# Splitting expert weights in a fused attention and MLP kernel: 24-bit words, rounded by ScalarE, low part by subtraction

## The chip, the cores and the metric

The kernel runs on one core of one Trainium2 chip. The metric is the device time of one launch in microseconds. A core has five engines with a queue each: TensorE (PE, matmuls; its weight loads are listed apart as PEld), VectorE (DVE), ScalarE (ACT), GpSimd (POOL) and SyncE (SP, which here only starts DMAs). Each engine works through its own instructions in order, and engines wait for each other on semaphores.

## The reference

Sink-window attention feeds a two-layer MLP with a squared ReLU.

```python
scores = (1.0 / np.sqrt(D)) * np.matmul(q, k.transpose(0, 1, 3, 2))   # q, k, v: (4, 8, 768, 64)
keep = is_sink | in_window                        # 4 sink keys, a causal window of 128
scores = np.where(keep, scores, -1000000000.0)
scores = scores - np.max(scores, axis=-1, keepdims=True)
a = np.exp(scores)
a = a / (np.sum(a, axis=-1, keepdims=True) + 1e-09)
x = np.matmul(a, v)                               # laid out as (3072, 512)
h = np.maximum(x @ w_in, 0.0)                     # w_in (512, 2048)
out = (h * h @ w_out).astype(np.float32)          # w_out (2048, 512), result (3072, 512)
```

The weights `w_in` and `w_out` arrive as float64 and are read by the kernel as pairs of 32-bit words: `low` (word 0) and `top` (word 1, with sign, exponent and the upper mantissa). 1e-9 is `EPS` in the kernel.

## The kernel before, in words

The 3072 tokens are eight chunks of 384; a chunk has four pairs of heads. For each pair, `score` (L233) makes scores on PE, takes the masked row maximum on DVE (the custom operation of L261, called the reduction here) and the exponential with its row sum on ACT (L264). `normalise` (L268) adds `EPS` to the sums, takes the reciprocal on DVE (L278) and lets POOL scale the probabilities (L289) and copy the sink columns (L302, L303). A tail then transposes the probabilities on PE (L358), copies them out of PSUM on ACT (L365) or DVE (L363), and does the same for the sink keys (`sink_keys`, L313, L314). `values` (L391) multiplies by v (L406, L409) and splits the result into a high part (ACT, L417) and a low part (DVE, L418).

`moe` (L453) yields the MLP in quanta, four to a block of 128 hidden columns: twelve matmuls of the first layer (L465), ReLU and squares on ACT (L476, L479, L481), a low part of the squares on DVE (L488), nine matmuls of the second layer (L503). Each weight is used as a high and a low part, both of the type fp32r, so a weight must be split before its first use.

`split_steps` (L564) splits one row, 128 partitions by 512 weights; there are 32 rows, 16 of each matrix, in the list `order`. A row is loaded by `load_row` (L558) into one of four buffers, two rows ahead. Before the change the row takes five passes on DVE and two on ACT:

- L573 and L575 (DVE): the top word is shifted and its sign and exponent bits are put back, which gives a float32 with 11 mantissa bits, `t1`;
- L577 (ACT) and L578 (DVE): the remaining bits are gathered as two 16-bit halves into an integer `m`;
- L580 (DVE): the exponent of `t1` alone, `eb`;
- L586 (ACT): `t1` is copied as the high part; L587 (DVE): the low part is `m * 2^-36 * eb`.

The order of the work is set in three ways. Up to the end of the first MLP leg (chunk 0, blocks 0 to 7) PE, DVE, ACT, POOL and SP follow the program's own order (`manual_schedule`). First come the pairs of chunk 0, `s` = 0 to 3, and a first pair of chunk 1, `s` = 4; between their parts `fill(1)` runs one step of the splitting, a step ending at each `yield`: fifteen such steps, five to a row before the change. To keep PE occupied there, `busy` (L638) issues matmuls on a zero tile. Then follows the loop of 32 quanta (`QUANTA`), called the loop here: each takes one quantum of the MLP, one item of the attention of chunk 1 (`todo`), and `fill(3)` or `fill(2)` steps of splitting. By its end 17 rows (`EARLY`) are split. After that, the other 15 rows (`split_row`, L590), the rest of the MLP and the attention of chunks 2 to 7 are ordered by the tile framework's planner by priorities.

Of the kernel before, what the change touches and what calls it, by code (L numbers as in the profile page):

```python
# [8 lines left out]
F32 = mybir.dt.float32  # L9
F32R = mybir.dt.float32r  # L10
I32 = mybir.dt.int32
U16 = mybir.dt.uint16
U32 = mybir.dt.uint32
BF16 = mybir.dt.bfloat16
AF = mybir.ActivationFunctionType
ALU = mybir.AluOpType
# [3 lines left out]
P = 128  # L20
# [6 lines left out]
WR = 512  # L27
# [7 lines left out]
EPS = 1.0e-9  # L35


def f32(ap):
    return ap.bitcast(F32)
# [3 lines left out]
def sink_window_attention_moe(  # L43
# [11 lines left out]
    nc = tc.nc  # L55
    B, NPAIR, _, S = q.shape
# [12 lines left out]
    with ExitStack() as fast:  # L69
        wp = fast.enter_context(tc.tile_pool(name="wp", bufs=1))  # L70
        ap1 = fast.enter_context(tc.tile_pool(name="ap1", bufs=1))
# [3 lines left out]
        op = fast.enter_context(tc.tile_pool(name="op", bufs=3))  # L75
# [23 lines left out]
        nc.gpsimd.iota(coli, pattern=[[1, P]], base=0, channel_multiplier=0)  # L99
        rel = op.tile([P, 2 * P], F32, tag="ob", name="rel")  # L100
        nc.vector.tensor_copy(rel, reli)
        far = ap1.tile([P, 2 * P], F32, tag="m", name="far")
        nc.vector.tensor_scalar(far, rel, 0.0, BIG, op0=ALU.is_lt, op1=ALU.mult)
        nc.vector.tensor_tensor(rel, rel, far, op=ALU.max)
        col = mp.tile([P, P], F32, tag="gl", name="col")
# [162 lines left out]
        def normalise(c, p, heads):  # L268
            st = state[c, p]
            half = c % NHALF  # L270
            i0 = 1 if half == 0 else 0
            hs = slice(heads[0], heads[-1] + 1)
            rs = ap2.tile([P, 2, NQ], F32, tag="rs", name=f"rs_{c}_{p}_{heads[0]}")
            if c > 1:
                nc.scalar.activation(rs[:, hs], st["sm"][:, hs], AF.Copy, bias=EPS)
            else:
                nc.vector.tensor_scalar(rs[:, hs], st["sm"][:, hs], EPS, None, op0=ALU.add)
            nc.vector.reciprocal(rs[:, hs], rs[:, hs])  # L278
            for hh in heads:
                Pt = st["P"][hh]  # L280
                j0 = 1 if half == 0 else 0
                if c > 1:

                    nc.gpsimd.tensor_tensor(  # L284
                        Pt[:, j0:NQ, 0:P], Pt[:, j0:NQ, 0:P], Pt[:, j0:NQ, BS:BAND], op=ALU.add
                    )
                for j in range(NQ):
                    n = P if j < j0 else (BS if c > 1 else BAND)
                    nc.gpsimd.tensor_scalar(  # L289
                        Pt[:, j, 0:n], Pt[:, j, 0:n], rs[:, hh, j : j + 1], 1.0, op0=ALU.mult, op1=ALU.mult  # L290
                    )
                own = slice(hh * NS, hh * NS + NS)
                src = Pt[:, i0:NQ, P:BS]
                if c > 1 and half == 1:

                    to = PSK[0].rearrange("p q c -> p (q c)")[:, 0 : NQ * 4 * NS]
                    to = to.rearrange("p (q t c) -> p q t c", t=2, c=2 * NS)
                    nc.gpsimd.tensor_copy(to[:, :, 0, own], src)
                    nc.gpsimd.tensor_tensor(to[:, :, 1, own], src, f32(to[:, :, 0, own]), op=ALU.subtract)
                    continue  # L300
                to = PSK[p % 2 if c < 2 else 0].rearrange("p q (t c) -> p q t c", c=2 * NS)[:, 0 : NQ - i0]
                nc.gpsimd.tensor_copy(to[:, :, 0:3:2, own], src.unsqueeze(2).broadcast_to([P, NQ - i0, 2, NS]))  # L302
                nc.gpsimd.tensor_tensor(to[:, :, 1, own], src, f32(to[:, :, 0, own]), op=ALU.subtract)  # L303
# [245 lines left out]
        NROW = len(order)  # L549
        HALF = NROW // 2  # L550
        AHEAD = 2
        raws = {}
# [5 lines left out]
        def load_row(n):  # L558
            if n in raws or n >= NROW:
                return  # L560
            raws[n] = wp.tile([P, WR, 2], I32, tag=f"wo{NFC - 4 + n % 4}", name=f"raw_{n}")
            nc.sync.dma_start(out=raws[n].rearrange("p (a w) t -> p a (w t)", a=NCC), in_=row_of(n))

        def split_steps(n):  # L564
            kind, j = order[n]
            load_row(n)
            top = raws[n][:, :, 1]
            words = raws[n].rearrange("p w t -> p (w t)").bitcast(U16).rearrange("p (w t) -> p w t", t=4)
            t1 = ap2.tile([P, WR], I32, tag="t1", name=f"t1_{n}")
            m = ap1.tile([P, WR], I32, tag="m", name=f"m_{n}")  # L570
            eb = ap1.tile([P, WR], I32, tag="eb", name=f"eb_{n}")
            m16 = m.bitcast(U16).rearrange("p (w t) -> p w t", t=2)
            nc.vector.tensor_scalar(t1, top, 3, 0x3FFFF000, op0=ALU.logical_shift_left, op1=ALU.bitwise_and)  # L573
            yield
            nc.vector.scalar_tensor_tensor(t1, top, -0x40000000, t1, op0=ALU.bitwise_and, op1=ALU.bitwise_or)  # L575
            yield
            nc.scalar.copy(m16[:, :, 0], words[:, :, 1])  # L577
            nc.vector.tensor_scalar(m16[:, :, 1], words[:, :, 2], 0x1FF, None, op0=ALU.bitwise_and)  # L578
            yield
            nc.vector.tensor_scalar(eb, t1, -0x800000, None, op0=ALU.bitwise_and)  # L580
            yield
            if kind == "i":
                row = wi[:, j]
            else:
                row = wo[j] = wp.tile([P, 2, DM], F32R, tag=f"wo{j}", name=f"wo_{j}")
            nc.scalar.copy(row[:, 0, :], f32(t1))  # L586
            nc.vector.scalar_tensor_tensor(row[:, 1, :], m, 2.0**-36, f32(eb), op0=ALU.mult, op1=ALU.mult)  # L587
            load_row(n + AHEAD)

        def split_row(n):  # L590
            keep = tc.cur_priority
# [5 lines left out]
        def check_row(n):  # L597

            keep = tc.cur_priority
            half = ap2.tile([P, WR // 2, 2], I32, tag="t1", name=f"half_{n}")  # L600
            sq = ap1.tile([P, WR // 2], BF16, tag="m", name=f"sq_{n}")
            src = row_of(n // 2)[:, n % 2 * 2 : n % 2 * 2 + 2]
            nc.sync.dma_start(out=half.rearrange("p (a w) t -> p a (w t)", a=2), in_=src)
            tc.cur_priority = keep + 12
            first = nc.scalar.activation(sq, f32(half[:, :, 1]), AF.Square, accum_out=wchk[:, 0, n : n + 1])
            tc.keep_in_program_order(first)
            nc.scalar.activation(sq, sq, AF.Relu, bias=theta, scale=-1.0, accum_out=wchk[:, 1, n : n + 1])
            tc.cur_priority = keep
# [4 lines left out]
        split = []  # L613

        def row_steps():
            for n in range(NROW):
                yield from split_steps(n)
                split.append(n)
                yield

        FH = NFC // 2
        legs = [(0, 0, FH), (1, 0, FH), (0, FH, NFC), (1, FH, NFC)] + [(c, 0, NFC) for c in range(2, NCHUNK)]
# [2 lines left out]
        EARLY = HALF + 1  # L625
        with tc.manual_schedule(engines={E.PE, E.DVE, E.Activation, E.Pool, E.SP}):
            steps = row_steps()

            def fill(n):
                for _ in range(n):  # L630
                    if len(split) < EARLY:
                        next(steps)
# [103 lines left out]
            for n in range(QUANTA):  # L736
                next(products)

                if todo:
                    todo.pop(0)()  # L740
                fill(3 if n % 4 == 0 else 2)
            while len(split) < EARLY:
                next(steps)
            for f in todo:
# [273 lines left out]
```

## Time and profile before

| | before |
|---|---|
| device time, median of 3 runs | 701.94 us (700.20 to 702.62) |
| device time of the profiled execution | 702.43 us |
| its span, first to last instruction | 700.7 us |
| PE busy / DVE busy / ACT busy / POOL busy | 686.8 / 430.5 / 439.3 / 228.1 us |
| granted TensorE clock, mean | 0.997 of full speed |

The profile lists for each engine its instructions with start, duration and, in square brackets, the idle time before it and what ended that. Durations of neighbours on one engine overlap a little at their ends, so the distance of two starts is what an instruction costs its queue. PE counts as busy also while a matmul waits inside its pipeline, so PE's share of busy time does not show by itself that it is at its limit.

### The profile page before, as it was taken

The numbers are of one execution on the slowest core, as the hardware profiler recorded it, in microseconds if no ns is written. First come the engines' busy times: TensorE is split into PE (matmuls) and PEld (weight loads), VectorE is DVE, ScalarE is ACT, GpSimd is POOL, SyncE is SP. The second block draws the span as 40 slices with busy tenths as digits, with TensorE's granted clock in tenths as the row PEclk, the third lists the DMA queues.
The fourth block names the chain that finished last, engine by engine and source line by source line (L and its number), as shares of the span: only waits on it lengthen the run. The fifth ranks groups of instructions, "written<-read, shape, count | busy, mean of one in ns | idle before, by whom it ended". The sixth has DMA issues, their size and how long they took to land.

```text
span 700.7 us, 11725 instructions
## 1 busy us (share of the span) xinstructions
PE 686.8 (98%) x3862; PEld 594.1 (85%) x3862; DVE 430.5 (61%) x1181; ACT 439.3 (63%) x1240; POOL 228.1 (33%) x433
## 2 busy tenths in 40 slices
PE   9899999999999999999999999999999999999995
PEld 4667789998888888888889888888988889889994
DVE  7789889946667666565566665666556665542221
ACT  6788877845666766676667777667676544422221
POOL 5664400034564432342343443233244242200000
PEclk9999999999999999999999999999999999999998
DMA  7476656511424423332435432243443210010001
GB/s 211 134 239 188 183 191 208 171 50 61 131 74 141 103 82 106 108 111 83 118 91 148 125 90 85 85 139 95 114 100 79 75 44 15 1 37 10 1 0 51
DMA packets 47268, 71.51 MB, mean 102 GB/s; under 512 B 4384, under 2 KB 30752, under 8 KB 47200
## 3 DMA queue, kind: packets, MB, share of 16 engines
q1 hardware_dynamic: 47056, 70.55, 34.8%
q8 instruction: 33, 0.54, 0.3%
q14 instruction: 35, 0.29, 0.1%
q10 hardware_dynamic: 144, 0.13, 0.1%
HBM read 62.80 MB, written 7.86 MB: 101 GB/s over the span
## 4 chain that ended last, share of the span: by engine, by line
PE 86%; ACT 2%; DVE 0%; issue 0%
PE po L503 36%; PE ph L465 36%; PE xo L406 5%; PE s L257 5%; PE pt L376 2%; PE xo L409 1%; ACT PTF L365 0%; ACT m L577 0%; ACT P L264 0%; PE pt L358 0%; PE pss L317 0%; PE pss L323 0%; ACT ph L481 0%; ACT ph L476 0%; ACT wi L586 0%
## 5 line engine op out<-in xcount | busy, mean ns | idle before, releaser
L465 PE MATMUL ph<-x,wi 128*128 128x384 f32 x1536 | 305.8, 340 | 0.0
L465 PEld LDWEIGHTS ph<-x,wi 128*128 128x128 f32 x1536 | 265.1, 188 | 9.1 <-issue 1.0
L503 PE MATMUL po<-wo,gh 128*128 128x512 f32 (+1 forms) x770 | 244.2, 398 | 0.0
L225 POOL TENSOR_TENSOR KS<-kn,KS 128x408 fp32r<-128x408 f32 (+1 forms) x48 | 58.8, 1226 | 317.8 <-ACT KS L224 317.8
L503 PEld LDWEIGHTS po<-wo,gh 128*128 128x128 f32 x770 | 136.0, 188 | 19.1 <-issue 1.6
L503 PE MATMUL po<-wo,gl 128*128 128x512 f32 x385 | 151.6, 394 | 0.0
L264 ACT ACTIVATE P<-P,nbs 128x264 f32<-128x264 f32 (+1 forms) x192 | 94.3, 491 | 74.3 <-DVE nbs L261 73.8
L484 DVE TENSOR_TENSOR ph<-ph,r 128x384 f32<-128x384 f32 x96 | 54.0, 563 | 76.7 <-ACT r L476 76.6
L261 DVE CUSTOM_DVE_ANT_0 P<-s,masks 128x264 f32<-128x264 f32 x160 | 67.1, 430 | 52.3 <-PE s L257 49.5
L289 POOL TENSOR_SCALAR P<-P,rs 128x136 f32<-128x136 f32 (+2 forms) x192 | 88.2, 475 | 31.6 <-DVE rs L278 23.4
L476 ACT ACTIVATE r<-ph 128x384 f32<-128x384 f32 x96 | 46.8, 487 | 77.6 <-PE ph L465 74.9
L503 PEld LDWEIGHTS po<-wo,gl 128*128 128x128 f32 x385 | 72.2, 188 | 16.1 <-DVE gl L488 0.2
L488 DVE TENSOR_TENSOR gl<-ph,gh 128x384 fp32r<-128x384 f32 x128 | 71.1, 555 | 23.5 <-ACT ph L481 12.0
L227 DVE TENSOR_TENSOR QS<-qn,QS 64x384 fp32r<-64x384 f32 x48 | 44.3, 922 | 24.4 <-ACT QS L226 24.0
L257 PE MATMUL s<-KS,QS 128*128 128x264 f32 (+1 forms) x288 | 56.9, 280 | 0.0
L284 POOL TENSOR_TENSOR P<-P 128x256 f32<-128x256 f32 (+1 forms) x48 | 48.4, 1009 | 24.9 <-ACT P L264 24.4
L257 PEld LDWEIGHTS s<-KS,QS 128*128 128x128 f32 x288 | 51.9, 188 | 5.0 <-DVE nbs L261 0.5
L479 ACT ACTIVATE gh<-r 128x384 fp32r<-128x384 f32 x96 | 50.3, 524 | 2.1
L382 DVE TENSOR_TENSOR PTF<-pt,halves 128x256 f32<-128x256 f32 x96 | 36.3, 419 | 22.1 <-PE pt L376 21.5
L406 PE MATMUL xo<-PTF,vn 128*64 128x256 f32 x448 | 45.9, 342 | 0.5 <-ACT PTF L365 0.5
L406 PEld LDWEIGHTS xo<-PTF,vn 128*64 128x64 f32 x448 | 31.2, 136 | 17.2 <-issue 9.3
L224 ACT CAST KS<-kn 128x408 fp32r<-128x408 f32 (+1 forms) x48 | 28.2, 589 | 24.5 <-issue 12.2
(108 smaller groups left out, 674.5 us busy)
## 6 DMA issues: line engine op xcount, KB each, us to landing
raw<-in_moe_w_in_dram SPq DMA_DIRECT2D x16, 512.0 KB, 3.9
raw<-in_moe_w_out_dram SPq DMA_DIRECT2D x16, 512.0 KB, 3.8
half<-in_moe_w_in_dram SPq DMA_DIRECT2D x32, 256.0 KB, 2.8
half<-in_moe_w_out_dram SPq DMA_DIRECT2D x32, 256.0 KB, 3.7
kn<-in_k_dram SPq DMA_DIRECT2D x24, 272.0 KB, 4.2
qn<-in_q_dram SPq DMA_DIRECT2D x32, 192.0 KB, 3.7
out_dram<-ob SPq DMA_DIRECT2D x23, 256.0 KB, 2.5
kn<-in_k_dram SPq DMA_DIRECT2D x24, 204.0 KB, 3.6
```

Source lines behind the costliest of these rows:

```text
L225: nc.gpsimd.tensor_tensor(KS[:, 1, 0:nk], st["kn"][:, hh, 0:nk], f32(KS[:, 0, 0:nk]), op=ALU.subtract)
L257: nc.tensor.matmul(ps[:, 0:n], st["QS", hh][:, qcols], flat[:, a, c0 : c0 + n], start=(a == 0), stop=(a == 1))
L261: nc.vector.tensor_tensor_reduce(Pt[:, i, 0:n], ps[:, 0:n], mask[:, 0:n], -SCALE, BIG, ALU.add, ALU.min, nb)
L264: nc.scalar.activation(Pt[:, i, 0:n], Pt[:, i, 0:n], AF.Exp, bias=nb, scale=-1.0, accum_out=sm[:, i : i + 1])
L284: nc.gpsimd.tensor_tensor(Pt[:, j0:NQ, 0:P], Pt[:, j0:NQ, 0:P], Pt[:, j0:NQ, BS:BAND], op=ALU.add)
L289: nc.gpsimd.tensor_scalar(Pt[:, j, 0:n], Pt[:, j, 0:n], rs[:, hh, j : j + 1], 1.0, op0=ALU.mult, op1=ALU.mult)
L406: nc.tensor.matmul(xo[h * D : h * D + D, cols], lhsT, rhs, start=(n == 0), stop=False, skip_group_check=True)
L465: nc.tensor.matmul(ph[:, 0:TOK], wi_at(i, cc, fc), xt[:, cc, :], start=(m == 0), stop=(m == 3 * NCC - 1),)
L479: nc.scalar.activation(gh, r, AF.Square)
L484: nc.vector.tensor_tensor(ph[:, 0:TOK], ph[:, 0:TOK], r, op=ALU.mult)
L488: late = lambda: nc.vector.tensor_tensor(gl, ph[:, 0:TOK], f32(gh), op=ALU.subtract)
L503: nc.tensor.matmul(po[t][:, e], gt[:, ts_], wo[f][:, i, e], start=(f == f0 and j == 0), stop=(f == f1 - 1 and j == 2), skip_group_check=True,)
```

## The change

The row is split in another way. The top word is shifted and masked with three more bits kept (L573's successor), the sign and exponent are put back as before, and a third pass joins the upper three bits of the low word, shifted right by 29: `t1` is now a float32 word with all 24 bits. ACT's copy of `t1` to fp32r rounds it, and the low part is the difference of the word and its rounded high part, a subtraction on DVE. So a row takes four passes on DVE and one on ACT; the tiles `m` and `eb` of the splitting are gone, and the two small users of the buffer tag `m` get a tag of their own (`far`).

A row now has four steps. `row_steps` is written anew: the first step of a row comes before the last step (the subtraction) of the row ahead of it. The load of the row two ahead is issued in the third step. The number of steps for each quantum goes from three in the first of four and two in the others (nine in four) to one in the last of four and two in the others (seven in four). In `normalise`, `EPS` is added by ACT for all chunks; before, DVE did it for chunks 0 and 1.

```diff
-            if c > 1:
-                nc.scalar.activation(rs[:, hs], st["sm"][:, hs], AF.Copy, bias=EPS)
-            else:
-                nc.vector.tensor_scalar(rs[:, hs], st["sm"][:, hs], EPS, None, op0=ALU.add)
+            nc.scalar.activation(rs[:, hs], st["sm"][:, hs], AF.Copy, bias=EPS)
             nc.vector.reciprocal(rs[:, hs], rs[:, hs])
...
-            nc.vector.tensor_scalar(t1, top, 3, 0x3FFFF000, op0=ALU.logical_shift_left, op1=ALU.bitwise_and)
+            nc.vector.tensor_scalar(t1, top, 3, 0x3FFFFFF8, op0=ALU.logical_shift_left, op1=ALU.bitwise_and)
             yield
             nc.vector.scalar_tensor_tensor(t1, top, -0x40000000, t1, op0=ALU.bitwise_and, op1=ALU.bitwise_or)
             yield
-            nc.scalar.copy(m16[:, :, 0], words[:, :, 1])
-            nc.vector.tensor_scalar(m16[:, :, 1], words[:, :, 2], 0x1FF, None, op0=ALU.bitwise_and)
-            yield
-            nc.vector.tensor_scalar(eb, t1, -0x800000, None, op0=ALU.bitwise_and)
-            yield
+            nc.vector.scalar_tensor_tensor(t1, low, 29, t1, op0=ALU.logical_shift_right, op1=ALU.bitwise_or)
...
             nc.scalar.copy(row[:, 0, :], f32(t1))
-            nc.vector.scalar_tensor_tensor(row[:, 1, :], m, 2.0**-36, f32(eb), op0=ALU.mult, op1=ALU.mult)
             load_row(n + AHEAD)
+            yield
+            nc.vector.tensor_tensor(row[:, 1, :], f32(t1), f32(row[:, 0, :]), op=ALU.subtract)
...
         def row_steps():
-            for n in range(NROW):
-                yield from split_steps(n)
-                split.append(n)
+            last = iter(())
+            for n in range(EARLY):
+                row = split_steps(n)
+                next(row)
                 yield
+                for _ in last:
+                    pass
+                if n > 0:
+                    split.append(n - 1)
+                    yield
+                next(row)
+                yield
+                next(row)
+                yield
+                last = row
+            for _ in last:
+                pass
+            split.append(EARLY - 1)
+            yield
...
-                fill(3 if n % 4 == 0 else 2)
+                fill(1 if n % 4 == 3 else 2)
```

More of the change, by code (lines that the diff above doesn't have):

```diff
@@ L101, in sink_window_attention_moe @@
         nc.vector.tensor_copy(rel, reli)
-        far = ap1.tile([P, 2 * P], F32, tag="m", name="far")
+        far = ap1.tile([P, 2 * P], F32, tag="far", name="far")
         nc.vector.tensor_scalar(far, rel, 0.0, BIG, op0=ALU.is_lt, op1=ALU.mult)
@@ L566, in split_steps @@
             load_row(n)
-            top = raws[n][:, :, 1]
-            words = raws[n].rearrange("p w t -> p (w t)").bitcast(U16).rearrange("p (w t) -> p w t", t=4)
+            top, low = raws[n][:, :, 1], raws[n][:, :, 0]
             t1 = ap2.tile([P, WR], I32, tag="t1", name=f"t1_{n}")
[L570 to L573, printed above, removed]
+            nc.vector.tensor_scalar(t1, top, 3, 0x3FFFFFF8, op0=ALU.logical_shift_left, op1=ALU.bitwise_and)
             yield
@@ L600, in check_row @@
             half = ap2.tile([P, WR // 2, 2], I32, tag="t1", name=f"half_{n}")
-            sq = ap1.tile([P, WR // 2], BF16, tag="m", name=f"sq_{n}")
+            sq = ap1.tile([P, WR // 2], BF16, tag="far", name=f"sq_{n}")
             src = row_of(n // 2)[:, n % 2 * 2 : n % 2 * 2 + 2]
```

## The prediction, made before the changed kernel ran

> **What bounds the kernel now.** I read the stretches first, since a share over the whole span mixes phases with different limits. The columns are PE, weight loads, DVE, ACT, POOL, each busy us (instructions), then clock, DMA share and GB/s.
>
> ```profile
> 37.00:92.00 55.00, 52.34 (x306) 40.41 (x304) 50.66 (x127) 47.24 (x113) 26.96 (x42) 1.00 0.65 197
> 92.00:137.00 45.00, 44.95 (x235) 40.45 (x236) 42.37 (x96) 34.94 (x69) 0.00 (x0) 1.00 0.59 192
> 137.00:692.00 555.00, 554.83 (x3128) 491.89 (x3127) 310.01 (x850) 330.63 (x980) 179.27 (x334) 1.00 0.29 81
> ```
>
> From 92 us to 692 us PE stands idle for 0.05 + 0.17 us of 600. The other 15 rows are split in 92 to 137 us with DVE at 42.37 of 45, and still PE doesn't wait. So what the change does to DVE and ACT there is worth nothing; the work behind 92 us only moves with its start. What can change the time lies before 92 us, in two stages. The loop of 32 quanta runs from about 37 to 92 us: PE is idle for 55 - 52.34 = 2.66 us, DVE is at 92%, ACT at 86%. Who PE and its weight loads wait for, in 36 to 92 us (us in total, times, longest):
>
> ```profile
> PE pt L358 <- ACT PTF L365: 1.2, 3, 0.4
> PE s L253 <- DVE nbs L261: 0.9, 1, 0.9
> PE pt L358 <- ACT SK L314: 0.2, 1, 0.2
> PEld s L253 <- DVE nbs L261: 2.9, 6, 1.3
> PEld pt L358 <- ACT PTF L365: 2.0, 3, 0.7
> PEld pt L358 <- ACT SK L314: 0.6, 1, 0.6
> ```
>
> And one at the loop's end:
>
> ```profile
> PE xo L406 <- ACT PTF L365: 0.5, 1, 0.5
> ```
>
> PE is held by ACT's copies out of PSUM and by DVE's reductions, because both engines are late. The matmul rows give a floor of 1.2 + 0.2 + 0.5 + 0.9 = 2.8 us; the weight loads' rows, which count waits that running matmuls partly cover, give with the last one a ceiling of 2.0 + 0.6 + 2.9 + 0.5 = 6.0 us. More than that can't be won in the loop.
>
> Before 37 us PE has little to do (its queue holds matmuls on a zero tile), and the start of the first MLP matmul, at 36.88 us, hangs on the chain DVE, ACT, DVE, POOL, PE. There a DVE pass can cost its full length.
>
> **The change, part by part.** The prices of the passes (busy us, mean ns; shapes are 128 by 512):
>
> ```profile
> L573 DVE TENSOR_SCALAR t<-raw 128x512 int32<-128x512 int32 x32 | 14.4, 453 | 0.0
> L575 DVE SCALAR_TENSOR_TENSOR t<-raw,t 128x512 int32<-128x512 int32 x32 | 23.0, 720 | 0.3
> L578 DVE TENSOR_SCALAR m<-raw 128x512 uint16<-128x512 uint16 x32 | 14.6, 456 | 0.0
> L580 DVE TENSOR_SCALAR eb<-t 128x512 int32<-128x512 int32 x32 | 14.8, 461 | 0.0
> L587 DVE SCALAR_TENSOR_TENSOR wi<-m,eb 128x512 fp32r<-128x512 int32 x16 | 11.1, 692 | 1.0 <-ACT m L577 0.5
> L577 ACT COPY m<-raw 128x512 uint16<-128x512 uint16 x32 | 24.9, 779 | 5.2 <-DVE wi L587 1.9 <-DVE wo L587 1.2 <-issue 1.2
> L586 ACT CAST wi<-t 128x512 fp32r<-128x512 f32 x16 | 9.9, 618 | 0.9 <-DVE t L575 0.8
> L277 DVE TENSOR_SCALAR rs<-sm 128x6 f32<-128x6 f32 x8 | 1.3, 169 | 2.9 <-ACT P L264 2.9
> ```
>
> A row costs DVE 0.453 + 0.720 + 0.456 + 0.461 + 0.692 = 2.78 us now. The new third pass has the form of L575, so 0.720. The subtraction isn't in the trace; two SBUF operands of this size with an fp32r result is L587, 0.692. So 0.453 + 0.720 + 0.720 + 0.692 = 2.59 us. One pass fewer is therefore worth only 0.2 us: two cheap passes go, and a dear one comes. ACT goes from 0.779 + 0.618 = 1.40 to 0.618 us a row.
>
> The subtraction's other bound is a two-operand DVE instruction that runs beside POOL's:
>
> ```profile
> L227 DVE TENSOR_TENSOR QS<-qn,QS x48: 551/966/1348, 74.1 to 587.2; 64x384 fp32r<-64x384 f32 x48
> ```
>
> Its median is 966 ns against a minimum of 551. At 966/551 the subtraction would be 1.21 us. I take 0.692: L575 and L587 have two SBUF operands too, run in the same stage with POOL busy for 26.96 of 55 us, and stay at 0.69 to 0.72 on average.
>
> The Trainium skill, "SBUF — State Buffer", section "Who interferes with whom", says that a DVE instruction with two SBUF inputs contends with a GpSimd instruction that reads SBUF, and that the later one blocks fully; it speaks against a row whose two-input passes rise from two to three. By it the subtraction is dear where POOL runs; with 1.21 us the fourteen subtractions of the loop would cost 14 x 0.52 = 7.3 us more on DVE and eat the gain below. L227 bears it out, L575 in this loop much less.
>
> *First stage, fifteen steps.* Before they are three rows, 3 x 2.78 = 8.3 us of DVE; after, with four steps a row, four first passes, eight two-operand ones and three subtractions: 1.8 + 5.8 + 2.1 = 9.7 us. What of the 1.4 us lies on the chain is seen at pair `s` = 2, whose end gates pair 3:
>
> ```profile
> 22.97 0.19 ACT L264 ACTIVATION_READ_ACCUMULATOR P<-P,nbs 128x1 f32 x1
> 23.19 0.17 DVE L277 TENSOR_SCALAR rs<-sm 128x6 f32<-128x6 f32 x1 [0.81 <-ACT P L264]
> 23.39 0.19 DVE L278 RECIPROCAL rs<-rs 128x6 f32<-128x6 f32 x1
> 23.50 0.65 DVE L587 SCALAR_TENSOR_TENSOR wi<-m,eb 128x512 fp32r<-128x512 int32 x1
> 25.20 0.41 DVE L573 TENSOR_SCALAR t<-raw 128x512 int32<-128x512 int32 x1
> 25.53 0.28 DVE L261 CUSTOM_DVE_ANT_0 P<-s,mask 128x128 f32<-128x128 f32 x1
> ```
>
> From the reciprocal on, DVE runs without a gap up to the reductions of pair 3 (25.53). Two steps lie in that run. The first (23.50) stays a two-operand pass of 0.65 us. The second (25.20), 0.41 us, becomes the third pass of row 2, again 0.65: +0.24. The step before the add fills a wait of 0.81 us and is free. For `EPS` by ACT the later chunks show the hand-over:
>
> ```profile
> 178.55 0.19 ACT L264 ACTIVATION_READ_ACCUMULATOR P<-P,nbs 128x1 f32 x1
> 178.83 0.20 ACT L275 ACTIVATE rs<-sm 128x3 f32<-128x3 f32 x1
> 179.07 0.18 DVE L278 RECIPROCAL rs<-rs 128x3 f32<-128x3 f32 x1 [1.14 <-ACT rs L275]
> ```
>
> From the end of the last row sum to the reciprocal it is 0.33 us there, against 0.23 us now: +0.10 for pair 2 and again for pair 3. Behind this add on ACT wait the copies of L417 and L365, some 0.3 us later; the DVE steps ahead of their readers cover that. Pair 3's reciprocal releases POOL, and this is tight:
>
> ```profile
> 29.36 1.83 POOL L289 TENSOR_SCALAR P<-P,rs 128x128 f32<-128x128 f32 x3 [0.34 <-DVE rs L278]
> 36.88 1.20 PE L465 MATMUL ph<-x,wi 128*128 128x384 f32 x6
> ```
>
> POOL waits for it already, PE's sink keys (L313) and tail for POOL, and the first MLP matmul comes behind. So it starts 0.24 + 0.10 + 0.10 = 0.44, about **0.5 us** later. Bounds: 0, if a less occupied ACT shortens the row of exponentials, and 1.0, if the two longer steps in pair 3 count too.
>
> One new wait is hidden. Step 4 is now the first pass of row 1, ahead of pair 0's reciprocal, and row 1 lands late:
>
> ```profile
> 5.31 0.59 SPq L562 DMA_DIRECT2D raw<-in_moe_w_in_dram  x1
> raw<-in_moe_w_in_dram SPq DMA_DIRECT2D x1, 512.0 KB, 5.7
> 10.52 0.19 DVE L278 RECIPROCAL rs<-rs 128x6 f32<-128x6 f32 x1
> 15.65 2.32 PE L642 MATMUL idle<-idle 128*128 128x512 bf16 x10
> 23.79 2.10 POOL L289 TENSOR_SCALAR P<-P,rs 128x128 f32<-128x128 f32 x3 [3.29 <-DVE rs L278]
> ```
>
> Issued at 5.31 us, it lands 5.7 us later, at 11.0. DVE waits for it, and the reciprocal comes behind that 0.4 us pass, at 11.4 instead of 10.52 us, and POOL with it: 0.9 us late. PE's zero-tile matmuls up to 17.97 us and POOL's pause of 3.29 us cover this; with no cover it would be 0.9 us. The row loads are issued a step earlier on SP, ahead of later q and k loads; no DVE wait for a row stands in the trace, so I cost that at nothing, covered by two rows of lead.
>
> *The loop.* Fourteen rows fall in it now: DVE 14 x 2.78 = 38.9, ACT 14 x 1.40 = 19.6 us. After, the steps 16 to 68 remain, 13 first passes, 26 two-operand and 14 subtractions: 5.9 + 18.7 + 9.7 = 34.3 us of DVE, and 13 x 0.618 = 8.0 of ACT. With four adds of 0.169 gone too, DVE has 5.3 us less of 50.66 and ACT some 11 less of 47.24. What reaches PE: of the waits for ACT I take the visible ones, 1.2 + 0.2 + 0.5 = 1.9 us, since ACT loses a quarter of its work just ahead of those copies. Of those for DVE, between 0.9 and 2.9, I take 1.1: its work shrinks by a tenth only. Together **-3.0 us**.
>
> *Sum.* +0.5 - 3.0 = -2.5 us on the profiled execution, 702.43 us (span 700.7 and 1.73 around it): 699.9. The median of the runs, 701.94, is 0.49 below that execution, so 699.4 us as a median.
>
> **The rivals.**
>
> *Nothing reaches PE.* The copies come earlier, but then wait for DVE, which keeps pace with the program; the floor of 2.8 us hardly moves, and the 0.5 us stays: 702.4. For it: DVE loses little. Against: PE's largest waits name ACT.
>
> *All of it reaches PE.* The ceiling, with half the loss: 701.94 - 6.0 + 0.2 = 696.1. Against: PE needs scores before DVE can reduce, so some of these waits are latency.
>
> *Slower: a lockstep of ACT and DVE.* ACT's copy of L586 now stands directly behind the DVE pass that makes its input, where before it was two steps away, and the subtraction needs that copy one step later. ReLU, squares and PSUM copies queue behind it on ACT, and PE waits for those. At the same place of the program the two engines stand apart now:
>
> ```profile
> 50.23 0.80 ACT L577 COPY m<-raw 128x512 uint16<-128x512 uint16 x1
> 51.65 0.45 DVE L578 TENSOR_SCALAR m<-raw 128x512 uint16<-128x512 uint16 x1
> 52.45 0.52 ACT L264 ACTIVATE P<-P,nbs 128x264 f32<-128x264 f32 x1 [1.42 <-DVE nbs L261]
> 63.56 0.45 DVE L578 TENSOR_SCALAR m<-raw 128x512 uint16<-128x512 uint16 x1
> 64.27 0.79 ACT L577 COPY m<-raw 128x512 uint16<-128x512 uint16 x1
> ```
>
> ACT leads by 1.42 us in one place and lags by 0.71 in another; the middle is a lead of 0.35. It then waits 0.35, 0.6 for the pass, and copies for 0.5: 1.45 us, where the two removed or moved ACT instructions took about 1.15. That is 0.30 us later a row, 13 x 0.30 = 3.9 us, less 1.1 from DVE, plus 0.5: 705.2. It decides from a lead of some 0.05 us on, if PSUM copies follow closely. Against it: where ACT leads most it stands idle right after in any case (1.42 us at 52.45).
>
> *Slower: dear subtractions.* If POOL's instructions stretch all fourteen subtractions in the loop to 1.21 us, as they do L227, DVE has 34.3 + 7.3 = 41.6 us there instead of 38.9 + 0.7, two more, and is the bound: ACT's relief is lost behind it, and 701.94 + 0.5 + 2.0 = 704.4. Against: L575 beside the same POOL work.
>
> That the change doesn't remove the passes is not in question; the text of the kernel shows it.
>
> **How the numbers follow.** About 0.3%, 2.1 us, is what a measurement of this kernel can tell from no change. Chances: forecast 0.48, with a range of its own of 697.6 to 701.2 and three parts in five of it below 699.8; nothing reaches PE 0.18; all of it 0.16; lockstep 0.13; dear subtractions 0.05. Faster is then 0.29 + 0.16 = 0.45, the same 0.19 + 0.18 = 0.37, slower 0.18. The range takes in the ceiling and goes part of the way to the lockstep: 696.0 to 704.0 us.
>
> **What would show it.** In the changed profile the subtraction should take 0.69 us and its median stay below 0.9; the first L465 matmul should start at 37.2 to 37.6 us; PE's idle time in the loop should fall from 2.7 to below 1 us, with the waits for L365 nearly gone; from the loop's end to the end of the span everything should take as long as now, 600 us nearly without idle PE. It is wrong if ACT's longest new wait is for the third pass with PE's waits for L365 as long as before, or if PE is idle behind 92 us, where the planner's order might have changed.

## The result and the profile after

The changed kernel takes 705.46 us (median of 6 runs, 704.11 to 705.92) against 701.53 us before in the same comparison (6 runs, 700.20 to 702.62): a ratio of 1.0054, 95% interval 1.0040 to 1.0068. It is slower by 3.9 us, where 2.5 us were forecast as a gain. The profiled execution took 705.92 us, with a span of 704.2 us.

The line numbers move by three: the MLP matmul L465 is now L462, the PSUM copies L365 and L314 are L362 and L311. The passes of a row are L566, L568 and L570, ScalarE's rounding copy is L575, the subtraction L578. First the stretches, with the columns of the prediction's first fence.

```profile
37.00:92.00 55.00, 51.02 (x299) 38.57 (x299) 44.54 (x108) 37.19 (x98) 26.00 (x42) 1.00 0.60 187
92.00:137.00 45.00, 45.00 (x241) 40.39 (x240) 43.48 (x82) 26.80 (x56) 0.00 (x0) 1.00 0.59 191
137.00:692.00 555.00, 554.82 (x3129) 492.05 (x3129) 308.90 (x849) 331.22 (x982) 178.21 (x334) 1.00 0.29 82
```

VectorE and ScalarE are both less busy in the loop than before (44.54 against 50.66 us, and 37.19 against 47.24), and yet PE is idle longer: 3.98 us against 2.66. Behind 92 us PE stands idle for 0.18 us, against 0.22 before. So the loss lies before 92 us, and it isn't work: it is waiting. The prices of the passes (busy us, mean ns | idle time ahead of them and what ended it) agree with that:

```profile
L570 DVE SCALAR_TENSOR_TENSOR t<-raw,t 128x512 int32<-128x512 int32 x32 | 23.1, 723 | 0.4
L568 DVE SCALAR_TENSOR_TENSOR t<-raw,t 128x512 int32<-128x512 int32 x32 | 22.2, 700 | 0.1
L566 DVE TENSOR_SCALAR t<-raw 128x512 int32<-128x512 int32 x32 | 13.3, 422 | 0.9 <-DMA raw<-in_moe_w_in_dram 0.9
L578 DVE TENSOR_TENSOR wi<-t,wi 128x512 fp32r<-128x512 f32 x16 | 11.4, 711 | 0.9 <-ACT wi L575 0.9
L575 ACT CAST wo<-t 128x512 fp32r<-128x512 f32 x16 | 9.9, 620 | 8.9 <-DVE t L570 8.5
L575 ACT CAST wi<-t 128x512 fp32r<-128x512 f32 x16 | 9.9, 619 | 10.3 <-DVE t L570 10.3
```

Each pass costs about what was forecast. What is new stands at the end of the last two rows: the copy waited 18.8 us for the third pass; before, the same copy (L586) waited 0.8 for its input, by the row that the prediction shows. The waits of the loop, 36 to 92 us (us in total, times, longest):

```profile
ACT wi L575 <- DVE t L570: 8.2, 7, 2.1
ACT wo L575 <- DVE t L570: 3.2, 3, 1.4
DVE x L415 <- ACT x L414: 6.9, 4, 2.4
DVE wo L578 <- ACT wo L575: 1.2, 3, 0.5
DVE wi L578 <- ACT wi L575: 0.7, 2, 0.4
PE pt L355 <- ACT SK L311: 2.9, 2, 1.6
PE s L253 <- DVE nbs L261: 0.5, 1, 0.5
PE ph L462 <- DVE gl L485: 0.5, 1, 0.5
PE xo L403 <- ACT PTF L362: 0.2, 1, 0.2
```

ScalarE waits 11.4 us for the third pass. In the other direction VectorE waits 6.9 us for ScalarE's copy of `x`; in the kernel before that row reads:

```profile
DVE x L418 <- ACT x L417: 2.6, 4, 1.3
```

PE's waits for the transposed probabilities' copies (`PTF`) have nearly gone, 0.2 instead of 1.2 + 0.5 us, as was hoped; in their place it waits 2.9 us for the sink keys' copy (`SK`). One such place in time (start, length, engine, idle before and releaser):

```profile
46.65 0.49 PE L310 MATMUL pss<-ident,PSK 128*64 128x128 f32 x3
...
47.52 0.86 DVE L570 SCALAR_TENSOR_TENSOR t<-raw,t 128x512 int32<-128x512 int32 x1
...
48.41 0.62 ACT L575 CAST wi<-t 128x512 fp32r<-128x512 f32 x1 [1.40 <-DVE t L570]
...
48.94 0.47 ACT L473 ACTIVATE ph<-ph 128x384 f32<-128x384 f32 x1
...
50.24 0.47 ACT L311 CAST SK<-pss 48x384 fp32r<-48x384 f32 x1
...
50.76 0.66 PE L355 MATMUL pt<-ident,P 128*128 128x128 f32 x4 [1.64 <-ACT SK L311]
```

ScalarE stands still for 1.40 us in front of the rounding copy. Behind it in its queue are ReLU, the squares and the `SK` copy. The input of that copy was ready when L310 ended, at 47.1 us; it starts at 50.24, and PE waits 1.64 us for it.

In the first stage the same happens. Two timelines, before and after, at the third query block of pair 3:

```profile
24.42 0.58 ACT L365 COPY PTF<-pt 128x512 f32<-128x512 f32 x1
...
25.33 1.15 PE L253 MATMUL s<-kn,qn 64*128 64x264 f32 x6 [0.57 <-DVE PTF L363]
...
26.41 1.30 PE L406 MATMUL xo<-PTF,vn 128*64 128x256 f32 x12
```

```profile
25.62 0.62 ACT L575 CAST wo<-t 128x512 fp32r<-128x512 f32 x1 [1.69 <-DVE t L570]
...
26.15 0.58 ACT L362 COPY PTF<-pt 128x512 f32<-128x512 f32 x1
...
26.78 1.10 PE L253 MATMUL s<-kn,qn 64*128 64x264 f32 x4 [1.02 <-ACT PTF L362]
...
27.80 2.40 PE L403 MATMUL xo<-PTF,vn 128*64 128x256 f32 x12
```

The `PTF` copy starts 1.73 us later because the rounding copy ahead of it waited 1.69 us. The values matmuls then take 2.40 us instead of 1.30: the granted clock is down, as the stretch from 27.00 shows (clock 0.50, third from the end).

```profile
23.60:27.00 3.40, 1.65 (x8) 0.81 (x8) 3.11 (x13) 1.71 (x5) 3.25 (x7) 1.00 0.79 267
27.00:30.40 3.40, 3.40 (x17) 1.82 (x16) 1.77 (x7) 2.70 (x13) 1.41 (x5) 0.50 0.00 1
```

The MLP matmuls of the whole run, before and after (ns min/median/max, first and last start in us):

```profile
L465 PE MATMUL ph<-x,wi x1536: 331/337/447, 36.9 to 688.6; 128*128 128x384 f32 x192
```

```profile
L462 PE MATMUL ph<-x,wi x1536: 331/337/446, 38.6 to 692.0; 128*128 128x384 f32 x192
```

The first starts 1.7 us later and the last 3.4 us later. In these two profiled executions half of the delay has arisen before the first MLP matmul and half behind it. The experiments below show that the early half is not what the loss hangs on.

### The profile page after: what moved, and what is told of

Its sections match the earlier page's. It is cut to its first block, busy times and chain, and to the rows that moved or that the text cites. A ratio compares the mean times of both kernels' runs of the same rounds, so it can differ in the third digit from the quotient of the medians.

```text
span 704.2 us, 11619 instructions
## 1 busy us (share of the span) xinstructions
PE 688.6 (98%) x3861; PEld 594.8 (84%) x3862; DVE 425.2 (60%) x1141; ACT 421.1 (60%) x1216; POOL 226.4 (32%) x433
## 4 chain that ended last, share of the span: by engine, by line
PE 89%; DVE 4%; ACT 3%; POOL 1%; DMA 1%; issue 1%; SPq 1%; DVEq 0%
PE ph L462 37%; PE po L500 36%; PE xo L403 6%; PE s L257 5%; PE pt L373 2%; PE xo L406 2%; DVE t L570 1%; DVE t L568 1%; ACT P L264 1%; DMA raw<-in_moe_w_in_dram 1%; POOL P L286 1%; PE s L253 1%; DVE P L261 1%; DVE x L415 0%; ACT x L414 0%
## 5 line engine op out<-in xcount | busy, mean ns | idle before, releaser
L462 PE MATMUL ph<-x,wi 128*128 128x384 f32 x1536 | 306.0, 340 | 0.5 <-DVE gl L485 0.5
L462 PEld LDWEIGHTS ph<-x,wi 128*128 128x128 f32 x1536 | 265.0, 188 | 9.8 <-issue 1.4
L225 POOL TENSOR_TENSOR KS<-kn,KS 128x408 fp32r<-128x408 f32 (+1 forms) x48 | 58.5, 1218 | 320.7 <-ACT KS L224 320.7
L286 POOL TENSOR_SCALAR P<-P,rs 128x136 f32<-128x136 f32 (+2 forms) x192 | 84.9, 458 | 33.5 <-DVE rs L275 26.5
```

The lines of the kernel that those rows point to most:

```text
L225: nc.gpsimd.tensor_tensor(KS[:, 1, 0:nk], st["kn"][:, hh, 0:nk], f32(KS[:, 0, 0:nk]), op=ALU.subtract)
L286: nc.gpsimd.tensor_scalar(Pt[:, j, 0:n], Pt[:, j, 0:n], rs[:, hh, j : j + 1], 1.0, op0=ALU.mult, op1=ALU.mult)
L462: nc.tensor.matmul(ph[:, 0:TOK], wi_at(i, cc, fc), xt[:, cc, :], start=(m == 0), stop=(m == 3 * NCC - 1),)
```

## The experiments

The leading theory was the lockstep: ScalarE's copy stands directly behind the pass that makes its input, ScalarE waits there, and the PSUM copies behind it come late. The rivals were VectorE's own work (one two-operand pass more on the chain), the hand-over of the `EPS` addition to ScalarE, and the slow clock as a cost of its own. The waits in the table are those of the rounding copy for its pass plus those of the low part for ScalarE, summed over the rows of the waits in 7 to 100 us; PE busy is that of 37 to 92 us. Each ratio is taken to the kernel before, run beside it (its medians there were 701.3 to 702.0 us). Waits and PE busy come from one profiled execution each. In four of them, the copy one step later, the copy directly behind in the kernel before, the earlier input one step later and the three steps in the first rows only, the mean granted clock in 37 to 92 us is 0.97 (elsewhere 1.00), and PE at half clock counts as busy too.

| kernel | us | ratio (95%) | waits, us | PE busy, us |
|---|---|---|---|---|
| before | 701.53 | 1 | 0.5 | 52.34 |
| changed | 705.46 | 1.0054 (1.0040–1.0068) | 17.0 | 51.02 |
| copy one step later | 706.45 | 1.0064 (1.0050–1.0078) | 16.0 | 50.22 |
| copy of a constant | 700.13 | 0.9979 (0.9970–0.9988) | 0 | 54.31 |
| `EPS` by VectorE | 705.77 | 1.0059 (1.0045–1.0073) | 19.0 | 50.42 |
| four zero-tile matmuls | 704.78 | 1.0041 (1.0028–1.0055) | 17.3 | 51.04 |
| before, `EPS` by ScalarE | 702.29 | 1.0015 (1.0004–1.0027) | 0.4 | 52.05 |
| three steps behind | 700.47 | 0.9982 (0.9973–0.9991) | 0.6 | 53.73 |
| two steps behind | 700.73 | 0.9986 (0.9976–0.9996) | 3.6 | 53.73 |
| earlier input | 701.08 | 0.9991 (0.9980–1.0003) | 4.7 | 53.16 |
| before, copy directly behind | 709.07 | 1.0118 (1.0100–1.0136) | 20.5 | 46.80 |
| combined | 700.03 | 0.9986 (0.9975–0.9997) | 1.0 | 53.96 |
| earlier input, one step later | 703.30 | 1.0022 (1.0010–1.0033) | 7.6 | 51.46 |
| three steps in the first rows only | 704.92 | 1.0047 (1.0028–1.0066) | 14.3 | 51.40 |

**The wait taken away.** The copy keeps its place and its length, and reads a constant tile that is ready, so the high part is no longer that of the weights.

```diff
-            nc.scalar.copy(row[:, 0, :], f32(t1))
+            nc.scalar.copy(row[:, 0, :], halves.rearrange("p a c -> p (a c)"))
```

> The rounding copy stays in its place and its length but reads a constant tile of 128x512 in place of the joined words, so that it waits for no pass of VectorE; the high part of each split row is then that constant, so the products are not those of the weights. Lockstep theory: this takes away the wait alone: 701 to 703 us, first ph matmul at 36.9 to 37.6. Dear-passes theory: 705 to 706, since VectorE does the same. Hand-over theory (EPS by ScalarE in the first stage): at most 0.5 us better than the changed kernel.

It took 700.13 us, 5.3 less than the changed kernel, with every pass of VectorE and every copy of ScalarE still there. Its MLP matmuls and its loop:

```profile
L462 PE MATMUL ph<-x,wi x1536: 331/337/447, 37.3 to 686.2; 128*128 128x384 f32 x192
```

```profile
37.00:92.00 55.00, 54.31 (x329) 42.25 (x327) 48.53 (x112) 40.74 (x105) 29.43 (x42) 1.00 0.66 200
```

PE is idle for 0.69 us in the loop. The first MLP matmul starts 0.4 us later than before and the last 2.4 earlier. So the wait makes the loss: with every other part of the change still there, the kernel is faster than before. The time lies just below the 701 us that the lockstep theory gave as its lower end. Dear passes (705 to 706) fall, and so does the hand-over as the main cause.

**The copy one step later.** Only ScalarE's order is changed: the copy goes to the next row's first step, right ahead of the subtraction's step.

```diff
-            nc.scalar.copy(row[:, 0, :], f32(t1))
             load_row(n + AHEAD)
             yield
+            nc.scalar.copy(row[:, 0, :], f32(t1))
+            yield
             nc.vector.tensor_tensor(row[:, 1, :], f32(t1), f32(row[:, 0, :]), op=ALU.subtract)
...
                 next(row)
+                next(last, None)
                 yield
```

> Only ScalarE's rounding copy of a row is moved, to the next row's first step, one step behind the third pass that makes its input; VectorE's order is the same. Lockstep theory: the waits of the copy for the third pass (18.8 us in the changed kernel) fall below 5 us, the PSUM copies are on time again, the first ph matmul starts near 37.3 us instead of 38.6, the loop gives back some 1.5 us or more, and the time is 700 to 703 us. Dear-passes theory (VectorE's own work, one two-operand pass more, is what is late): the copy's place doesn't matter, 705 to 706 us, first ph matmul still at 38.3 or later. Third possibility: the subtraction, one step behind the copy, now waits for ScalarE, so that the wait only changes its engine: 704.5 to 706 us, with waits of the subtraction for the copy above 5 us.

It took 706.45 us. The waits are those of the third possibility, and the time lies 0.45 us above its range. The waits in 7 to 100 us (L577 is the copy, L579 the subtraction):

```profile
ACT wi L577 <- DVE t L570: 6.2, 5, 2.2
ACT wo L577 <- DVE t L570: 2.3, 3, 1.0
DVE wi L579 <- ACT wi L577: 4.1, 5, 1.3
DVE wo L579 <- ACT wo L577: 3.4, 4, 1.7
```

The copy's wait falls from 14.4 to 8.5 us, and the subtraction's rises from 2.6 to 7.5. One step isn't enough on the first side, since the longest wait is still 2.2 us; and on the other side only the first pass of a row, 0.42 us, is now left between the copy, 0.62 us, and the subtraction that reads it.

**Distance on both sides.** Two orders of the same instructions: the copy three steps behind the third pass and the subtraction two steps behind the copy; and two steps and one step. The copy's own move is the one shown above.

```diff
                 row = split_steps(n)
                 next(row)
                 yield
+                next(row)
+                next(last, None)
+                yield
+                next(row)
+                yield
                 for _ in last:
                     pass
                 if n > 0:
                     split.append(n - 1)
                     yield
-                next(row)
-                yield
-                next(row)
-                yield
                 last = row
```

> The rounding copy is issued three steps behind the third pass (in the next row's second step) and the subtraction two steps behind the copy, all instructions as in the changed kernel. Distance theory (the wait is real, and one step, about 1 us, isn't enough because ScalarE runs up to 2.2 us ahead of VectorE): copies wait under 3 us in all in 7 to 100 us, subtractions under 2 us, first ph matmul at 37.0 to 38.0, the time 699.5 to 702. Circle theory (two engines that hand a row to and fro wait for each other wherever the hand-over stands): the waits stay above 10 us together and the time above 704.

The second order takes the last `next(row)` and its `yield` behind the loop over `last`.

> The rounding copy is issued two steps behind the third pass, the subtraction one step behind the copy. Distance theory: the copies' waits fall (2 to 6 us), the subtractions' waits stay as in the kernel with the copy one step later (7.5 us), since their distance to the copy is the same: 702 to 705 us. Circle theory: 705 to 706.5.

They took 700.47 and 700.73 us. The only wait of the kind that is left with three steps, and its loop:

```profile
ACT wi L577 <- DVE t L570: 0.6, 1, 0.6
```

```profile
37.00:92.00 55.00, 53.73 (x328) 41.77 (x324) 48.84 (x111) 41.06 (x106) 28.27 (x42) 1.00 0.67 199
```

The first MLP matmul starts at 38.1 us with three steps, just behind the 37.0 to 38.0 expected and nearly as late as in the changed kernel, and yet the last starts at 687.7 us instead of 692.0. PE no longer waits for the `SK` copy, and VectorE's waits for `x` are halved; all that the view of 36 to 92 us lists for PE's matmuls, and that row of VectorE's, are:

```profile
PE s L253 <- DVE nbs L261: 0.7, 1, 0.7
PE xo L403 <- ACT PTF L362: 0.5, 1, 0.5
DVE x L415 <- ACT x L414: 3.5, 2, 2.1
```

The distance theory holds, and two engines that hand a row to and fro don't have to wait for each other. With two steps I had the subtraction wrong: forecast at 7.5 us of waits, it shows 1.1, and the time is below the 702 us that were expected. The copy, 0.62 us, now shares its step with a two-operand pass of 0.69 us; there it shared it with the pass of 0.42. That the longer pass covers the copy is argued from these lengths, not tested by itself. Both kernels are faster than before as well as than the change.

**The input made earlier.** The copy stays directly behind the third pass but reads the result of the second; the third pass writes a tile of its own.

```diff
-            nc.vector.scalar_tensor_tensor(t1, low, 29, t1, op0=ALU.logical_shift_right, op1=ALU.bitwise_or)
+            t2 = ap1.tile([P, WR], I32, tag="far", name=f"t2_{n}")
+            nc.vector.scalar_tensor_tensor(t2, low, 29, t1, op0=ALU.logical_shift_right, op1=ALU.bitwise_or)
...
-            nc.vector.tensor_tensor(row[:, 1, :], f32(t1), f32(row[:, 0, :]), op=ALU.subtract)
+            nc.vector.tensor_tensor(row[:, 1, :], f32(t2), f32(row[:, 0, :]), op=ALU.subtract)
```

> The rounding copy stays where it is, but reads the word after the second pass (21 bits of it; the third pass writes a tile of its own, from which the rounded part is subtracted, so the two parts still add up to the 24-bit word). It then waits for a pass that is one step, 1 us, earlier. By the waits: each of the twelve waits in 7 to 100 us shrinks by up to the 0.69 us of the third pass, so 14.4 us fall to 6 to 8, and the time to 702 to 704. If it is as with the copy issued one step later, 705.5 to 706.5.

701.08 us, better than the 702 to 704 expected: 4.1 us of the copy's waits are left, not 6 to 8. One step on this side, with the subtraction's distance untouched, wins 4.4 us, where the same step won by moving the copy lost it on the other side.

**The same input, with the copy one step later too.** The edit joins two diffs shown above, that of the earlier input and that of the copy one step later, and two shown below, `EPS` by VectorE and the zero-tile matmuls.

> Copy of the 21-bit word issued one step behind the third pass (two behind its own input), subtraction one step behind the copy, EPS by VectorE in the first two chunks, and the four zero-tile matmuls. If only the distance from input to copy counts: waits of the copy under 2 us, 699.5 to 700.6 us. If the subtraction, one step behind the copy, now waits instead: waits of the subtraction over 3 us and 701 to 703.

703.30 us. The subtraction waits 4.8 us, the copy 2.8: the rival expectation, 0.3 us above its range. Again only the 0.42 us pass stands between the copy and its reader.

**The lockstep put into the kernel before.** Its five passes stay; the rounding copy moves from the fifth step to the second, directly behind its input.

```diff
             nc.vector.scalar_tensor_tensor(t1, top, -0x40000000, t1, op0=ALU.bitwise_and, op1=ALU.bitwise_or)
+            if kind == "i":
+                row = wi[:, j]
...
+            nc.scalar.copy(row[:, 0, :], f32(t1))
             yield
...
-            nc.scalar.copy(row[:, 0, :], f32(t1))
             nc.vector.scalar_tensor_tensor(row[:, 1, :], m, 2.0**-36, f32(eb), op0=ALU.mult, op1=ALU.mult)
```

> The kernel before, with its five VectorE passes, and one thing changed: ScalarE's rounding copy is issued directly behind the second pass that makes its input, where it stood three steps later. If the place of the copy alone makes the wait, whatever the number of passes: new waits of the copy for the second pass of over 8 us in 7 to 100 us, and the time 703.5 to 706. If the old kernel has more slack on ScalarE's side than the changed one (its VectorE passes are shorter): under 4 us of waits, and 701 to 702.5.

709.07 us, 7.2 more than the kernel before, beyond the expected 703.5 to 706. Its waits in 7 to 100 us, the last of them that of the transposes for the copy of `PTF`:

```profile
ACT wo L580 <- DVE t L575: 8.6, 5, 2.3
ACT wi L580 <- DVE t L575: 6.4, 6, 2.3
DVE wi L587 <- ACT m L582: 5.5, 5, 2.6
...
PE pt L358 <- ACT PTF L365: 4.5, 3, 2.1
```

So the place of one ScalarE instruction makes a loss with five VectorE passes a row as well as with four. Here it also delays the 16-bit copy (L582) behind it, and VectorE's last pass waits 5.5 us for that.

**Where the price is paid.** Three steps behind for the first four rows, which fall in the first stage; directly behind for the others. The edit is shown against the kernel with three steps.

```diff
                 row = split_steps(n)
                 next(row)
                 yield
-                next(row)
-                next(last, None)
-                yield
-                next(row)
-                yield
+                if n < 4:
+                    next(row)
+                    next(last, None)
+                    yield
+                    next(row)
+                    yield
                 for _ in last:
                     pass
                 if n > 0:
                     split.append(n - 1)
                     yield
+                if n >= 4:
+                    next(row)
+                    yield
+                    next(row)
+                    next(row)
+                    yield
                 last = row
```

> The first four rows, which lie in the first stage, have the copy three steps behind the third pass; all later rows have it directly behind the third pass, as in the changed kernel. So it tells how the wait's price is shared. If the loop carries nearly all of it (TensorE's offset against the kernel before grew by 1.6 us in the loop of the changed kernel and fell by 2.1 with three steps, so 3.8 of some 5): first ph matmul at 36.9 to 38.2, waits of the copy in 7 to 100 us above 10 us, 704 to 705.5 us. If it is the first rows whose delay is dragged along: 701 to 703.

704.92 us, with 10.7 us of the copy's waits left; the first MLP matmul starts at 37.8 us. Against 700.47 with three steps in all rows, the loop's rows carry some 4.4 us, and giving the first four rows their distance wins 0.5 of the changed kernel's 705.46, which lies within the intervals. So it isn't a delay of the first rows that is dragged along: what they win ahead of the loop (a first start 0.8 us earlier than in the changed kernel) is lost again in it.

**EPS, alone and undone.** In the changed kernel VectorE adds `EPS` in the first two chunks again; in the kernel before ScalarE does it everywhere.

```diff
-            nc.scalar.activation(rs[:, hs], st["sm"][:, hs], AF.Copy, bias=EPS)
+            if c > 1:
+                nc.scalar.activation(rs[:, hs], st["sm"][:, hs], AF.Copy, bias=EPS)
+            else:
+                nc.vector.tensor_scalar(rs[:, hs], st["sm"][:, hs], EPS, None, op0=ALU.add)
```

> One part is undone: EPS is added by VectorE again in the first two chunks, all else as in the changed kernel. Lockstep theory: 0 to 0.5 us better, 705.0 to 705.5, first ph matmul at 38.3 to 38.6. Hand-over theory: the addition on ScalarE stands in front of the PSUM copies and behind the last exponential, and it alone is worth over 1.5 us: below 704.

> One part of the change alone, in the kernel before: EPS is added by ScalarE in all chunks, the split stays as it was. By the prediction's price (0.10 us twice in the first stage) 0 to 0.4 us slower, first ph matmul at 36.9 to 37.3, no measurable change. If the hand-over is dear where VectorE runs ahead or behind: over 1 us slower, waits of the reciprocal for ScalarE over 4 us.

Undone it gives 705.77 us, no gain, although the first MLP matmul starts at 37.7 us, ahead of the 38.3 to 38.6 expected. Alone it gives 702.29 (first start 35.8 us, where 36.9 to 37.3 were expected), a ratio of 1.0015 with an interval of 1.0004 to 1.0027, so 0.3 to 1.9 us slower, where 0 to 0.4 were expected; the reciprocal's waits for ScalarE are 6.0 us, above the 4 us of the rival expectation. What it costs by itself isn't settled by these two; it is not what makes the change slow.

**The slow clock.** Four more matmuls on the zero tile, ahead of the third query block of pair 3.

```diff
                 for i, tags in enumerate(trios):
+                    if s == 3 and i == 2:
+                        busy(4)
                     scores(s, i, tags, (0, 1) if s else (1,))
```

> The changed kernel with four more matmuls on the zero tile (0.23 us each) between the second and the third query block of pair 3's scores, where TensorE waits 1.02 us for ScalarE and after which the granted clock stands at 0.5 for 3.4 us. If the slow clock is a cost of its own: no 0.5 in the records, the values matmuls take 1.3 instead of 2.4 us, the first ph matmul starts 0.8 to 1.2 us earlier, at 37.4 to 37.8, and the time is 704.3 to 704.7. If TensorE's time there is hidden by GpSimd's scaling behind it: values fast again, but the first ph matmul at 38.5 and 705.5 us. If it is idle TensorE before the third block that counts, and not the clock: 705.5 to 706.

The two stretches with these matmuls:

```profile
23.60:27.00 3.40, 2.86 (x15) 1.22 (x14) 2.73 (x12) 1.77 (x6) 3.25 (x8) 1.00 0.88 268
27.00:30.40 3.40, 3.40 (x31) 2.75 (x30) 2.15 (x8) 3.37 (x14) 1.41 (x5) 1.00 0.31 92
```

The clock stays at 1.00, the values matmuls take 1.30 us again, and the first MLP matmul starts at 37.5 us, 1.1 earlier. The time is 704.78, 0.7 below the changed kernel; the two ratios' intervals overlap, so that the clock costs anything in the end isn't shown. It is in any case the lesser part: with `EPS` by VectorE the profile has no slow clock in 20 to 100 us, and the time is 705.77; with three steps it has one, from 27.40 to 30.82 us, and the time is 700.47.

**What can be had.** The diffs of three experiments above taken together: three steps behind, `EPS` by VectorE in the first two chunks, and the zero-tile matmuls.

> Copy three steps behind the third pass, subtraction two behind the copy, EPS by VectorE in the first two chunks, and four zero-tile matmuls before the third query block of pair 3. If the first stage's losses (hand-over, slow clock) add to the loop's gain: first ph matmul at 36.9 to 37.4, no 0.5 in the clock, 699.3 to 700.2 us. If they are taken up again in the loop, where another wait ends last: 700.3 to 700.9, as without them.

700.03 us, a ratio of 0.9986 (0.9975 to 0.9997) to the kernel before. The first MLP matmul starts at 36.2 us, earlier than expected, and no slow clock shows in 27 to 37 us, but the time can't be told from that with three steps alone. Both beat both kernels, by about 1 us against the one before (ratios of 0.9982 and 0.9986) and by about 5 against the changed one.

## Why the prediction was wrong

*The step that failed* is one that the sum did not hold. The rounding copy, which had two steps between itself and its input, was put directly behind it, and the sum gave this no term; it stood only as a rival, with a chance of 0.13. Taking away that wait alone moved the time by -5.3 us. The argument against the rival was that ScalarE stands idle anyway where it leads most (1.42 us at 52.45). That idle time does not absorb the new wait: in 36 to 92 us ScalarE's waits for the reductions fell only from 3.6 to 2.5 us, against 11.4 us of new ones. The place where ScalarE waits decides which copies stand behind it. At 52.45 it waited ahead of an exponential; in the place shown from the changed kernel, at 48.41, it waits ahead of ReLU, squares and a PSUM copy that PE needs. The prediction's sign of being wrong came by half: ScalarE's longest new wait is for the third pass, but PE's waits for the `PTF` copy did not stay as they were; they moved to the `SK` copy.

*The rival's size.* 705.2 us came within 0.3 of the result, but not by its terms. It took a lead of 0.35 us as the middle of two places; the twelve waits in 7 to 100 us have a mean of 14.4/12 = 1.2 us. Its 0.6 us for the pass, 0.5 for the copy and 1.15 for ScalarE's work before are not the 0.72, 0.62 and 1.40 of the rows of the passes; with these a row comes to 0.29 us where it had 0.30, since the errors cancel. It saw a late subtraction as the path back to VectorE; the larger path back is the copy of `x`, 6.9 us against 2.6. And it placed only 0.5 us in the first stage, where the first MLP matmul came 1.7 us late.

*First stage, +0.5 us.* In the changed kernel that matmul starts at 38.6, outside 37.2 to 37.6. With the wait gone it starts at 37.3, which is 0.4 late. The price of the dearer steps was right as far as this one start tells: in kernels whose times differ little it lies anywhere from 35.8 to 38.1 us. The new wait for row 1 came as worked out, and it was covered, since GpSimd still pauses for 2.13 us ahead of pair 2's scaling (3.29 before):

```profile
11.14 0.43 DVE L566 TENSOR_SCALAR t<-raw 128x512 int32<-128x512 int32 x1 [0.69 <-DMA raw<-in_moe_w_in_dram]
11.48 0.18 DVE L275 RECIPROCAL rs<-rs 128x6 f32<-128x6 f32 x1
```

The reciprocal at 11.48 instead of 10.52 was forecast at 11.4.

*The loop, -3.0 us.* By the MLP matmuls' starts, the kernel whose copy doesn't wait gains 0.4 + 2.4 = 2.8 us between the first and the last. These are two profiled executions; over all runs its ratio of 0.9979 (0.9970 to 0.9988) is a gain of some 1.5 us, 0.8 to 2.1, where 2.5 in all were forecast. ScalarE's lighter load does reach PE once nothing blocks its queue; in the changed kernel the same two starts give a loss of 1.7. With the copy three steps behind its input the median is 700.47 and with a constant as its input 700.13: both lie in the forecast's own range of 697.6 to 701.2, which was made for the changed kernel and did not hold it.

*Dear subtractions.* The subtraction's medians are 684 and 689 ns, forecast 692, and its longest 919 ns. The Trainium skill, "SBUF — State Buffer", section "Who interferes with whom", would have a two-input pass block beside GpSimd; with GpSimd busy for 26.00 of 55 us no such pass is dear on average here (0.72 to 0.78 us in the loop), so in this loop the trace doesn't bear the rule out as a price. Two single passes agree with it: the third pass that starts at 67.66 takes 1.28 us, the second pass at 75.08 takes 1.05, and each ends 0.55 to 0.56 us after an addition of GpSimd's (L225, from 67.33 to 68.39 and from 74.51 to 75.57 us) that had begun before it. No other two-input pass of a row in the loop took more than 0.92 us.

*Behind 92 us, nothing.* PE's idle time there is 0.18 us, against 0.22 before.

## What to carry to other kernels

On engines that take their queues in order, the distance between a producer on one engine and its reader on the other is a price of its own: cost an edit by which instruction now stands directly behind its input, and by what waits behind that instruction, before counting the work it saves. Measure how far one queue runs ahead of the other (here up to 2.2 us); a hand-over spaced by about that much waited little here (three steps, of some 1 us each, left 0.6 us of the copy's waits, two steps 2.5), and on the way back it paid to have as much work between as the other engine's instruction is long. Moving a wait by one step can hand it to the other engine; giving both sides room needs an order in which one row's halves are worked off beside the next row's.

## What the runs showed of the hardware

In the changed kernel a stretch in which PE was busy for 1.65 of 3.40 us was followed by 3.4 us at a granted clock of 0.50; with the four zero-tile matmuls PE was busy for 2.86 of 3.40 us there, and the clock stayed at 1.00. How long PE is busy does not decide it alone: with three steps a stretch with 2.30 of 3.41 us (23.99 to 27.40) was followed by the slow clock too, and in the changed kernel one with 1.77 of 3.41 us (47.46 to 50.87) was not. What decides stays open. The Trainium skill, "TensorE: Matmul & The Clock Gate", section "What's actually happening", has the clock halved after an idle window of some 3.4 us; the length agrees, but here the windows ahead of the slow clock were only partly idle.

The second thing is how little the wait shows where it acts: PE's visible waits in the loop rose by little more than 1 us (2.9 + 0.5 + 0.5 + 0.2 against 1.2 + 0.2 + 0.5 + 0.9), while taking the hand-over's 17.0 us of waits away (14.4 of ScalarE, 2.6 of VectorE) gave 5.3 us. That VectorE's waits for `x` pass part of it on is likely, since they rise from 2.6 to 6.9 us with the copy's waits and fall to 3.5 without them; how the rest is passed on was not followed instruction by instruction and stays open.
